# Twelve later row tiles normalised in the first part instead of six, leaf buffers fifteen instead of twelve, the second part's written order replaced

## The chip, the cores and the metric

The kernel runs on one core of one Trainium2 chip. Its engines work side by side, each through its own list of instructions in order: PE multiplies matrices (PEld, its weight load, runs beside it), ACT applies functions with a scale and an offset, DVE and POOL do elementwise arithmetic, and SP issues the transfers between DRAM and on-chip memory (DMA). Engines wait for one another through semaphores. PE writes its products into eight banks; ACT and DVE read them out, and a bank can be written again only then.

The metric is the time of one execution on the device, in microseconds (us): the median of several runs.

## The reference, cut to what matters

```python
# q, k, v: (8, 8, 576, 64); omega: (128, 64)
def phi(x):                       # x scaled by 64 ** -0.25
    h = einsum('bhsd,md->bhsm', x, omega) - sum(x * x, -1) / 2
    return exp(h - max(h, -1)) / sqrt(128)
q_p, k_p = phi(q_s), phi(k_s)
kv = einsum('bhsm,bhsd->bhmd', k_p, v); z = sum(k_p, 2)
attn = einsum('bhsm,bhmd->bhsd', q_p, kv) / (einsum('bhsm,bhm->bhs', q_p, z) + 1e-6)
x = attn with its heads side by side         # (8, 576, 512)
u = x + real(fft(fft(x, axis=1), axis=2))
un = (u - mean(u)) / sqrt(var(u) + 1e-6)     # along a row of 512
out = u + relu(un @ w_ch1) @ w_ch2           # 512 -> 2048 -> 512
```

All of it is float32. Batch and sequence together are 4608 rows of `u`.

## The kernel before

**Two parts.** The first part computes the attention, the Fourier mix (which stores `u` to the DRAM array `us`), the whole multilayer perceptron for the first 512 rows in four plain blocks of 128 rows (first layer L1235, second layer L1258), and conversions of the weights. The second part takes the other 4096 rows in eight blocks j = 0 to 7 of 512 rows with a two-level Strassen-Winograd scheme: each layer is 7 x 7 = 49 products ("leaves"). A leaf of a first layer is L1710, of a second layer L2153. Blocks 0 and 1 are worked alone, then 2 and 3, 4 and 5, 6 and 7 in pairs ("wide"), which share their weights. Every leaf of a second layer has a tile of weights `wl` of 256 KB, loaded from the array `w2l` (L2049) into one of 12 buffers (`NWL`). The sums of operand blocks that the scheme needs are additions at L1666, the ones that finish rows at L2202; each may be placed on DVE or on POOL. L2129 and its neighbours put leaf products together on DVE.

**Normalised, turned rows.** Blocks 1 to 7 need their rows normalised and transposed. A tile of 128 rows is loaded from `us`, ACT forms its mean and square sum in two passes, POOL makes the factor out of them in three tiny instructions, ACT scales, DVE transposes, and SP stores the result to an array `turned`, from which a block's fetch later reads its operand (L1091 for block 1, L1086 for wide blocks). There are two forms of this chain:

- *in the second part*: `normed` (L1096) lays out a block's tiles, `norm_of` (L1128) and `by_blocks` (L1058) make the instructions: load L1135 into one of two buffers `u`, ACT L1144 and L1149, POOL L1153 to L1155, ACT L1157, DVE L1068 into the buffer `turn`, store L1074. Blocks 1 to 7 have four tiles each.
- *in the first part*: the generator `ahead` (L1572) does the same for the tiles of the list `EARLY`: all four of block 1 and the first two of block 2. Its lines are load L1578, ACT L1582 and L1583, POOL L1585 to L1587, ACT L1589, DVE L1592, store L1594. A tile lies in one of the two buffers `kq` that hold keys and queries earlier on.

**The order.** The kernel's instructions are put into the queues by `Listing.run`. Each part is a set of streams (generators of steps). A step names its engine or engines, what it takes (buffers, banks) and what it waits for. Which stream is served next, and on which of its engines, is written out as text: `PICKS` and `BANKS` for the first part, `PICKS2` and `BANKS2` (three characters a step, one digit for each choice of bank) for the second. The generators of `ahead` are not in these lists. They are advanced by `BETWEEN`: groups of five digits, a count of placed steps and the number of a tile.

```python
            placed += 1
            while between and between[0][0] == placed:
                next(between.pop(0)[1], None)
```

At such a count the tile's next stage is put in the queues at that point: its load, its two ACT passes, its POOL triple, its scaling, its transpose, its store. An instruction that waits then holds up all that stands behind it on its engine. SP's queue is in order too.

**Work of the first part that the steps touch** (all near 350 to 420 us): attention forms `e` = exp on ACT (L650, eight instructions of 128x128), which PE transposes (L596). The Fourier mix has `y` on ACT (L906), read by PE at L933, and `bmp` (L977), which ACT copies out of a bank. The plain blocks write banks at L1235 and L1258, and ACT or DVE apply the relu (`ht`, L1221 and L1219). `u` rows are loaded at L1032.

## Time and profile before

| what | us |
| --- | --- |
| runs | 1128.26, 1128.29, 1128.4; median 1128.29 |
| the profiled execution | 1128.43 |
| its span, first to last instruction | 1126.6 |
| PE busy | 1108.2 (98%) |
| PEld busy | 1000.7 (89%) |
| DVE busy | 888.1 (79%) |
| ACT busy | 541.8 (48%) |
| POOL busy | 357.4 (32%) |
| moved by DMA | 236.11 MB, 210 GB/s over the span |

The profile is that of one execution; 1.8 us of its time lie outside the span. Busy shares are averages over parts with different limits, so the table says only that PE is nearly always at work: 18.4 us of the span are left in which it is not. The page's slices show where; its first and last lie at the start and the end of the program:

```
PE   8999999999999999999999999999999999999998
DMA  8956757565675549799899668757778756556553
```

Each digit is a fortieth of the span, 28 us, in tenths; 9 stands for 90% or more. Finer windows and the timeline of one engine follow in the prediction.

### The profile page before, as it was taken

The page shows a single profiled execution, that of the slowest core. Times are in us where ns is not written, and L with a number is a line of the kernel's source. Part 1 is how long each engine was busy: PE and PEld are TensorE (multiplying, and loading weights), DVE is VectorE, ACT ScalarE, POOL GpSimd, SP SyncE. Part 2 cuts the span into 40 slices and gives each one's busy share as a digit, 9 for nine tenths or more (in the row PEclk, how much of TensorE's full clock was granted, in tenths as well). Part 3 has the DMA queues.
Part 4 walks back from the last instruction along what each step waited for, and adds up shares of the span by engine and source line. Part 5 has one row for each costly group of instructions (what it writes and reads, how often), then busy time and mean ns, then how long its engine had stood idle before and what let it go on. Part 6 is the DMA issues. An engine that isn't in the chain of part 4 may idle for free.

```text
span 1126.6 us, 31534 instructions
## 1 busy us (share of the span) xinstructions
PE 1108.2 (98%) x12467; PEld 1000.7 (89%) x12467; DVE 888.1 (79%) x1705; ACT 541.8 (48%) x1644; POOL 357.4 (32%) x381
## 2 busy tenths in 40 slices
PE   8999999999999999999999999999999999999998
PEld 7878888879869779999999889999889999889998
DVE  6999998987577766497788777888667898668895
ACT  7998898856536335534313553223563222341221
POOL 2443443644473335434300454000365000142000
PEclk9999999999999999999999999999999999999999
DMA  8956757565675549799899668757778756556553
GB/s 236 234 178 180 238 174 211 165 206 165 219 234 183 156 137 350 209 292 293 225 317 323 188 204 267 205 151 226 214 208 258 216 152 219 167 156 215 150 157 106
DMA packets 194867, 236.11 MB, mean 210 GB/s; under 512 B 52128, under 2 KB 118944, under 8 KB 194720
## 3 DMA queue, kind: packets, MB, share of 16 engines
q1 hardware_dynamic: 194224, 233.83, 68.3%
q8 instruction: 99, 1.62, 0.6%
q14 instruction: 48, 0.39, 0.1%
q10 hardware_dynamic: 496, 0.26, 0.1%
HBM read 182.13 MB, written 56.10 MB: 211 GB/s over the span
## 4 chain that ended last, share of the span: by engine, by line
PE 90%; DMA 3%; DVE 3%; ACT 2%; SPq 1%; issue 0%; DVEq 0%; ACTq 0%
PE banks L2153 30%; PE banks L1710 27%; PE banks L690 5%; PE banks L1235 5%; PE banks L596 5%; PE banks L1258 5%; PE banks L1861 4%; PE banks L724 3%; PE banks L771 2%; PE banks L933 2%; PE banks L883 1%; DMA wl<-w2l 1%; DMA kq<-in_q_dram 1%; PE banks L893 1%; ACT e L650 1%; PE banks L944 1%
## 5 line engine op out<-in xcount | busy, mean ns | idle before, releaser
L2153 PE MATMUL banks<-wl,sums 128*128 128x128 f32 x1792 | 219.8, 275 | 0.0
L2153 PEld LDWEIGHTS banks<-wl,sums 128*128 128x128 f32 x1792 | 210.9, 192 | 0.9 <-issue 0.2
L650 ACT ACTIVATE e<-banks,nmx 128x128 f32<-128x128 f32 x576 | 165.3, 432 | 22.6 <-DVE nmx L633 22.0
L633 DVE TENSOR_REDUCE nmx<-banks 128x8 f32<-128x1024 f32 (+1 forms) x96 | 89.4, 952 | 19.1 <-PE banks L690 14.9
L2153 PE MATMUL banks<-wl,hid 128*128 128x128 f32 x768 | 99.2, 276 | 3.1 <-DMA wl<-w2l 1.8
L2153 PEld LDWEIGHTS banks<-wl,hid 128*128 128x128 f32 x768 | 92.6, 192 | 4.5 <-DVE part L2129 1.8
L2124 ACT ACTIVATE s<-banks 128x128 f32<-128x128 f32 x112 | 31.0, 277 | 121.1 <-PE banks L2153 111.5
L1710 PE MATMUL banks<-unw,wxw 128*128 128x256 f32 x352 | 85.5, 379 | 0.0
L690 PE MATMUL banks<-om,kqT 64*64 64x128 f32 (+1 forms) x2088 | 79.2, 275 | 1.5 <-ACT kv L740 0.8
L690 PEld LDWEIGHTS banks<-om,kqT 64*64 64x64 f32 (+1 forms) x2088 | 64.5, 138 | 12.7 <-issue 3.4
L2153 PE MATMUL banks<-wl,hx 128*128 128x128 f32 x576 | 74.2, 275 | 0.4 <-DVE part L2129 0.4
L1710 PEld LDWEIGHTS banks<-unw,wxw 128*128 128x128 f32 x352 | 66.6, 190 | 8.9
L1710 PE MATMUL banks<-rx,wxw 128*128 128x256 f32 x288 | 71.2, 379 | 0.0
L1710 PE MATMUL banks<-ttw,wxw 128*128 128x256 f32 x288 | 70.0, 379 | 0.0
L2153 PEld LDWEIGHTS banks<-wl,hx 128*128 128x128 f32 x576 | 69.4, 192 | 0.7 <-DVE part L2129 0.6
L1735 ACT ACTIVATE s<-banks 128x512 f32<-128x512 f32 x65 | 38.6, 595 | 60.0 <-PE banks L1710 54.8
L1235 PE MATMUL banks<-unT,w 128*128 128x128 f32 x512 | 65.4, 279 | 1.7 <-DVE qeT L610 1.7
L1235 PEld LDWEIGHTS banks<-unT,w 128*128 128x128 f32 x512 | 60.2, 192 | 4.5 <-issue 2.3
L539 POOL TENSOR_TENSOR w<-w,raw 128x512 f32<-128x512 f32 x28 | 37.4, 1343 | 76.6 <-DVE raw L533 76.6
L1710 PEld LDWEIGHTS banks<-rx,wxw 128*128 128x128 f32 x288 | 54.5, 190 | 7.3
L1710 PEld LDWEIGHTS banks<-ttw,wxw 128*128 128x128 f32 x288 | 54.5, 190 | 7.3
L1258 PE MATMUL banks<-w,ht 128*128 128x512 f32 x128 | 58.8, 598 | 0.0
(268 smaller groups left out, 2353.3 us busy)
## 6 DMA issues: line engine op xcount, KB each, us to landing
wl<-w2l SPq DMA_DIRECT2D x245, 256.0 KB
wxw<-w1x SPq DMA_DIRECT2D x120, 256.0 KB
raw<-in_moe_w_ch_dram SPq DMA_DIRECT2D x32, 512.0 KB
kq<-in_k_dram SPq DMA_DIRECT2D x32, 288.0 KB
kq<-in_q_dram SPq DMA_DIRECT2D x32, 288.0 KB
vd<-in_v_dram SPq DMA_DIRECT2D x32, 288.0 KB
u<-us SPq DMA_DIRECT2D x30, 256.0 KB
ur<-us SPq DMA_DIRECT2D x30, 256.0 KB
```

Of the source, the lines that this page charges most:

```text
L539: eng.tensor_tensor(out=dst, in0=dst, in1=lof, op=ALU.add)
L596: nc.tensor.transpose(ps[:, (j - j0) * 128 : (j - j0 + 1) * 128], src(j), ident[:])
L633: nc.vector.tensor_reduce(nmx[:, :, 0:num], pps[:, :, 0 : MF * num].rearrange("p b (c m) -> p b c m", m=MF), axis=AX.X, op=ALU.max, negate ...
L650: nc.scalar.activation(out=e[:, c + (i if num == 1 else 0), :], in_=pps[:, i, MF * c : MF * c + MF], func=AF.Exp, bias=nmx[:, i, c : c + 1],)
L690: nc.tensor.matmul(pps[cols, c, MF * m : MF * m + MF], lhsT=kqT[rows, j, cols], rhs=om2[rows, :],)
L724: nc.tensor.matmul(kvp[cols, i, 0 : D + 1], lhsT=feature(r)[rows, cols], rhs=vds[n % NV][rows, r, :], start=(r == 0), stop=(r == R - 1),)
L1235: nc.tensor.matmul(hp[:, 0:TP], lhsT=w1[:, dc, 128 * fc : 128 * fc + 128], rhs=unTs[key][:, dc, :], start=(dc == 0), stop=(dc == NDC - 1),)
L1258: nc.tensor.matmul(yp[:, 0:DM], lhsT=hs[fc][:, 128 * i : 128 * i + 128], rhs=w2[:, fc, :], start=(fc == 0), stop=(fc == NFC - 1),)
L1710: nc.tensor.matmul(ps[:, span * f : span * f + span].rearrange("f (b q) -> f b q", q=Q), lhsT=left[:, P * f : P * f + P], rhs=right, start ...
L1735: nc.scalar.activation(out=s[:], in_=ps, func=AF.Copy)
L1861: nc.tensor.matmul(cell.rearrange("f t (b q) -> f t b q", q=Q), lhsT=w[:, d, col : col + 128], rhs=right[:, :, d].rearrange("f (t b) q -> ...
L2153: nc.tensor.matmul(ps[:, 0:128], lhsT=left[:, f], rhs=wls[head(j), i, n][:, f], start=start and f == 0, stop=(f == 3), skip_group_check=True,)
```

## The change

Twelve tiles are in `EARLY`: all of blocks 1, 2 and 3. The list `PLACES` gives each of them a buffer: tiles 0, 1, 5, 6, 10 and 11 in the two `kq` buffers (`k`), tiles 2, 3, 4, 7, 8 and 9 in the three buffers of the tag `turned`, which hold turned keys in the attention (`t`). `BETWEEN` has groups for twelve tiles, the number being a hexadecimal digit, and places most stages of tiles 0 to 5 elsewhere than before. `normed` serves blocks 4 to 7 only, and its branches for blocks 1 to 3 are gone. Of the leaves of blocks 0 and 1 in the second layer, every fifth takes the place of a `u` buffer or of the `turn` buffer (`tag_of`), so that there are 12 + 2 + 1 buffers; wide blocks keep 12. The second part's order `PICKS2` and `BANKS2` is replaced whole. The first part's `PICKS` and `BANKS` stay.

In numbers of instructions: PE, ACT and SP have as many as before (of SP's, six loads and six stores come from L1578 and L1594 instead of L1135 and L1074); 21 additions of L1666 and L2202 go from DVE to POOL. PE's order is the same in the first part and in the last 1552 matmuls.

```diff
+PLACES = "kktttkktttkk"
 BETWEEN = (
-    "1662016621167001690116910169101693016991169911699117300173011750217502175031766317692176921769317773"
-    "17792177921790317903180341804518204182041820418205182051820518384183851846418465")
+    "1662016620166211670116910169101691116911169301693117300173011730217302174321743217503175031750417504"
+    "1750517506175821763217637176651766617693176931769417694176951769617713177131771817765177761777717794"
+    "17794177991785517855179061790617928179991803a1804b18057180571806818069181371813718168182091820a1820a"
+    "1820a1820b1820b1820b1824818248183491838a1838b184291846a1846b")
 PICKS2 = (
...
 BANKS2 = (
...
         def paced(i):
             h, k = divmod(i, HT // 128)
-            before, then = ((("first", j - 1, n[i], 0), "y") for n in ((1, 1, 5, 2), (6, 2, 7, 3)))
-            if wide(j):
-
-                n, was = i + TB // 128 * (j - head(j)), head(head(j) - 1)
-                order_ = [((("first",) + p), "y") for p in heads(was)]
-                at = [m * (len(order_) - 2) // 7 for m in range(8)]
-                if j <= WIDE + 1:
-                    order_ = [(("first", 0, 7, 0), "y"), *((("second", 0, k), "p1") for k in (4, 6))]
-                    order_ += [(("first", 1, ORDER1[k], 0), "y") for k in (0, 2, 4, 6)]
-                    at = range(-2, 6)
-                before, then = order_[at[n]], order_[at[n] + 1]
+
+            n, was = i + TB // 128 * (j - head(j)), head(head(j) - 1)
+            order_ = [((("first",) + p), "y") for p in heads(was)]
+            at = [m * (len(order_) - 2) // 7 for m in range(8)]
+            before, then = order_[at[n]], order_[at[n] + 1]
             yield Step(NONE, after=events_of(range(t0, t0 + TB // 128)) + (before,))
             yield from norm_of(j, t0 + 2 * h, i, pool, None, (h, k), (then,))
         for i in range(TB // 128):
-            if (j, i) in EARLY:
-                continue
-            if wide(j):
-                n = i + TB // 128 * (j - head(j))
-                was = head(head(j) - 1)
-                at = 98 * was + 49 * len(unit(was)) * n // 8 - 8
-                if j <= WIDE + 1:
-                    at = (0, 0, 28, 52, 73, 98, 112, 126)[n]
-                yield Fork(paced(i), LEAF * at)
-                continue
-            yield Fork(paced(i), LEAF * (98 * j - 60 + 8 * i))
+            n, was = i + TB // 128 * (j - head(j)), head(head(j) - 1)
+            yield Fork(paced(i), LEAF * (98 * was + 49 * len(unit(was)) * n // 8 - 8))
     def norm_of(j, t, i, pool, dst, block=None, after=()):
...
         h, k = divmod(i, HT // 128)
         t = (NPLAIN * TP + TB * j) // 128 + 2 * h
-        place = ld.tile([P, 2 * R, D], F32, name="kq", tag="kq")[:].rearrange("p c d -> p (c d)")
+        if PLACES[EARLY.index((j, i))] == "k":
+            place = ld.tile([P, 2 * R, D], F32, name="kq", tag="kq")
+        else:
+            place = att.tile([128, R, 128], F32, name="kqT", tag="turned")
+        place = place[:].rearrange("p c d -> p (c d)")
         u, w = place[:, 0:DM], place[:, DM : 2 * DM]
         nc.sync.dma_start(u, us[P * t : P * (t + 2), :].rearrange("(b k q) d -> k b q d", k=2, q=Q)[k])
         yield
...
         nc.sync.dma_start(turned_of(j, h)[:, :, k], turn.rearrange("p g d q -> p g (d q)"))
         listing.made["turned", j, i] = 0.0
-    EARLY = [(j, i) for j in (1, 2) for i in range(TB // 128)][:6]
+    EARLY = [(j, i) for j in (1, 2, 3) for i in range(TB // 128)]
     def betweens():
         tiles = [ahead(*n) for n in EARLY]
-        return [(int(BETWEEN[n : n + 4]), tiles[int(BETWEEN[n + 4])]) for n in range(0, len(BETWEEN), 5)]
+        return [(int(BETWEEN[n : n + 4]), tiles[int(BETWEEN[n + 4], 16)]) for n in range(0, len(BETWEEN), 5)]
     every = mybir.EngineType
     ctx.enter_context(
...
         return (4, 1, 2, 6, 5, 3, 7) if head(j) != head(NTB - 1) else (4, 1, 2, 6, 7, 5, 3)
+    def tag_of(j, i, l):
+
+        n = (49 * j + 7 * order(j).index(i) + PARTS.index(l)) % 15
+        if wide(j) or n % 5 != 4:
+            return "wl", NWL
+        return ("turn", 1) if n == 14 else ("u", 2)
+
     def load_leaves():
         for j in HEADS:
             for i in ORDER1[j == WIDE :] if wide(j) else ():
...
                     wxs[j, i, n] = wx
             for i in order(j):
                 for l in PARTS:
+                    tag, n = tag_of(j, i, l)
                     yield Step(
-                        SP, 0.45, 2.6, take=("wl",), after=(("w2l", i),), kb=165, makes=("wl", j, i, l),
+                        SP, 0.45, 2.6, take=(tag,), after=(("w2l", i),), kb=165, makes=("wl", j, i, l),
                         bias=due(j, 1, i) + (LEAF * 2 * PARTS.index(l) if wide(j) else 0.0) - 14,
                     )
-                    wl = late.tile([128, 4, 128], F32, name="wl", tag="wl", bufs=NWL)
+                    wl = late.tile([128, 4, 128], F32, name="wl", tag=tag, bufs=n)
                     nc.sync.dma_start(wl[:].rearrange("p f m -> p (f m)"), w2l[i][STORED.index(l)])
                     wls[j, i, l] = wl
...
                 0.895,
                 after=(("wl", head(j), i, n),) + shared + after,
                 take=take,
-                give=(() if wide(j) and j == head(j) else ("wl",)) + give,
+                give=(() if wide(j) and j == head(j) else tag_of(j, i, n)[:1]) + give,
                 makes=makes or (me, n), bias=pace * LEAF * PARTS.index(n),
             )
             b = None
...
             yield from block_norms(j, late)
     def late_turns():
-        for j in range(2, NTB):
+        for j in range(4, NTB):
             yield from normed(j, late)
     listing.run(
```

More of the change, by code (lines that the diff above doesn't have):

```diff
@@ L103 @@
 PICKS2 = (
-    "0260260270280000270290290290260280240261260290310251280251290450480490270451280230480420480290460440"
-    "2802602504812504802404704604504704504505105105103812605105002504102404912404804604604802304404904614"
-    "9150048048052053049052053053035044049046037052037041028046125037048044048038046037141154052043043060"
-    "0400370330330570540351230450370350360270440580570570470550261230420521230280360360480470400440470300"
-    "4603803504004202802905005605614815903905705312305906103405804905003705604905905403304903804803303905"
@@ L109 @@
-    "2058048051037033046051034039058051046059059025057046038033052035037055039060057043037047045054057045"
-    "0410440670571270670690530670440470400510470510490310600460390270390580380500611280630560590620410631"
-    "2715106104904706000005505005405405604315904004704314403205505305315405303204303805712615102603603914"
-    "2052040043038041153049064060053022049050040061039047063000050038040049052050051035129054022059137044"
-    "0500500370570320370200630560340480200440500471440590600600410580510360420490400550510520610471510590"
@@ L114 @@
-    "6203805106006205606005706015705805406115004216005203215606005915705105205405215604805405204804603815"
-    "6027022054049028148047043046051045053155147045047024053148043050153043046148021037047055056052037054"
-    "1490480520410430501470540470000551520470520490550571471531560470540440440540520490540480440450490320"
-    "5104603503914804704005105103204404604004304904405304704005104303304905013903905005104704005204604804"
-    "5051052053053053042145045046054141049046153040052040051051046047051048038053143147049053053053053045"
@@ L119 @@
-    "0410450240430430410001460420480270360481410440440380390500420400460440410450420310420480420520500440"
-    "4204503804205114903604003804703704004802103904504604701803903905403703605405405205605505503703403705"
-    "2055051051054053050053053050053055036029051050035051050044046048051051050046049053053046052044044034"
-    "0440480480450430470240320430460451540460460450500471490550410320400480450450000450460430390470470500"
-    "4504604104404002204904004702404504004811804004402104103604704503804004104204203502804804603404504704"
@@ L124 @@
-    "6048039039037044045042043044042034034040040045042040040039034000052032033044038033016032040027032037"
-    "0340430361250290380400330420320360370480390370460290420300350400500370251260490390170360370330410430"
-    "3303103203703603802304403803003604502403603504603303202504604103402304403403103003003202604113814103"
-    "3030032041032039026034030029127027131027036029027031041045041027029027034142143032020039037027036028"
-    "0270400400261340321270320260310310310370370350340300350300331310350340350390390390391360370260360300"
@@ L129 @@
-    "3012903703103103513113903403203303903403703203102903303602902313513402903313602403403203512803513403"
-    "2135032036033033133031030034032131030031032032132031034035128032028037032038035132032035032026026023"
-    "0300370161270251270270260360271321331360310250310290351300341311331340241330290350251320320290290180"
-    "2002201712503102102403102902402803203401803202803302503203112103012802102102203002802003102302702712"
-    "6020023026023023124023020023029017027122028027125024023026128030029024021029027021026023029027020125"
@@ L134 @@
-    "0230261210261301330250240240260240220320280220300300251250280220250190250300201200270000200260220220"
-    "2303303302602801902612402802702502401902912902802802102702402802002702602502302802102601702502102202"
-    "8018027026028020020127127127021018023024019000019025014017026027026018024026017014021016020017020016"
-    "022017016025024"
+    "0200220200000180190230220230200200240210200250240191251250230250230230230280440230220200170180420420"
+    "4302604004101801801801803512004103404003503412004104304204802303204603004502204403604303604501912004"
@@ new lines @@
+    "0031040119019031022036038030032032024045145045145049033122047036034039017047033042042048023046037045"
+    "0250360430270420190241411430421190450380360480320490330220250500500390360390410430480310340440430220"
+    "2804904402305403301803204003905304704802703101803903705303802805205303605004004304004805404903805305"
+    "3036047020046037048044117126039023032043042037024044026035044037043032051024025054019046046038119033"
+    "0530470520440350280440480280410490470471470190440420460441190460440460440480500400530310380250370380"
@@ new lines @@
+    "3903302505201904603804713504103502915004803413114803304404405014705302804002514214304314703004604702"
+    "1045043047029042029053045039052046045051029038038052050026037050049050046046049047051049041044151040"
+    "0400480430500490320210330451441350250381520440231510450290391510401530170350460430470360370500450521"
+    "4203615404804315004301604405204701905314604503804304905204714514904004201804804104114704714904404704"
+    "7050026146032020022045045036047017047045139021045028025033049042048042044035027047045031025031034040"
@@ new lines @@
+    "0380381360450320310370461460370400350420220420411301440390391390420400430220430451420440431390420380"
+    "3703703103704102203904304313803503303801603103403304104203203702403704103804204203504204104404403804"
+    "0139041037044139042040039039043036043038039033046046046046046046045033040039043136142042044040043039"
+    "0470360450310440470370420380410410420460460371370400410430440430400441250370340330340360430380360390"
+    "4003503404403903603905503905003705505505505005403404903504803514802704903204804904802004504105003105"
@@ new lines @@
+    "1048050048049052044046052043050041048044044031041042025042038016045046019040041042044037041044018049"
+    "0420460470420440390470370371420420350400360350380420450180430340400360360360350460340340390370370490"
+    "4205203404803604503503903704404304202905103404204102704003304705003504904504304804303104904704905003"
+    "0041043049036039047047047034043040042044029030038033035037041126020044036036033045034042043037041125"
+    "0440440390380480380410350310460250500450370380370310300260380350410340410450450450360440390360430430"
@@ new lines @@
+    "2803604103303903403703903504203003903603804203603603903203403403303903414013314202503202604103103913"
+    "7041031039042037038034042037031040035032035031031040131019034040131031034030026029038029039035038036"
+    "0330351320231370341311370341340270310280311311330380310391370340270280380290321360350330330380301300"
+    "2703512903703203203602813103102903313102703302703103703302703303213303413203402903613203503603602702"
+    "3127020131031134027019132032027025032033024028033128031029031021016032027029023029026033033132031127"
@@ new lines @@
+    "0270310290290270301251320190240221300301300240290310250280320270250240310281250280250271270300240220"
+    "2803003001702503002602402902002902603102202703002702902202502113113102802902802103202413002902903302"
+    "8024032017021016025026024000026030028033031029030017023024025025024029031031025030029021019027118022"
+    "0200310210330250240220281250270180230300300300300220310310270250200180000190180230210270250170180220"
+    "3002902402601801701502302202202301702402701801802802101901702302701602112001902102401801801502602702"
@@ L138 @@
+    "3021020030022028018020028015016015020015018033035032035018017019029014015027028015029015029000028030"
+    "030026025027026"
 )
 BANKS2 = (
-    "5670712567365475162765765076736574251742053164735260173564271706573527460152371054362071534267053152"
-    "76"
+    "5670512657367410557657657625754360671452603172465071374605263072645016472350473612540371645623701746"
+    "37125"
 )
```

## The prediction

> **What bounds the kernel now.** I read the windows first: the span cut into stretches, with each engine's busy time in each. The columns are: window, its length, then busy us (and instructions) of PE, PEld, DVE, ACT, POOL, the granted TensorE clock, the share of the DMA engines, GB/s.

> ```profile
> 350.00:375.00 25.00, 25.00 (x431) 20.37 (x432) 18.30 (x49) 14.59 (x52) 7.64 (x12) 1.00 0.50 175
> 375.00:400.00 25.00, 25.00 (x194) 19.68 (x189) 18.72 (x47) 10.41 (x35) 6.68 (x15) 1.00 0.44 125
> 400.00:425.00 25.00, 25.00 (x145) 16.73 (x144) 16.34 (x40) 9.34 (x23) 8.13 (x11) 1.00 0.55 159
> 475.00:500.00 25.00, 24.57 (x216) 24.03 (x214) 20.96 (x30) 7.87 (x29) 12.72 (x13) 1.00 1.01 284
> 500.00:525.00 25.00, 23.66 (x209) 23.47 (x210) 19.03 (x46) 9.27 (x24) 8.93 (x10) 1.00 0.93 277
> 575.00:600.00 25.00, 23.61 (x205) 23.16 (x204) 20.47 (x40) 4.91 (x19) 0.00 (x0) 1.00 0.97 327
> ```

> PE sets the time: it is busy 1108.2 us of a span of 1126.6, and its clock stands at 1.00. In 350 to 425, where the six added tiles go, PE never waits, and DMA stands at half. From 475 to 600, the second layers of blocks 0 and 1, PE loses 0.43 + 1.34 + 1.39 = 3.16 us, with DMA at 0.93 to 1.01: too many bytes. PE's timeline names the losses (start, length, engine, line, operation, in brackets the idle time before it and what ended it):

> ```profile
> 486.04 1.16 PE L2153 MATMUL banks<-wl,hid 128*128 128x128 f32 x8 [0.37 <-DMA wl<-w2l]
> ...
> 500.90 1.16 PE L2153 MATMUL banks<-wl,hid 128*128 128x128 f32 x8 [0.93 <-DVE part L2129]
> 502.50 2.05 PE L2153 MATMUL banks<-wl,hid 128*128 128x128 f32 x16 [0.44 <-DVE part L2129]
> ...
> 581.33 1.13 PE L2153 MATMUL banks<-wl,hid 128*128 128x128 f32 x8 [0.60 <-DMA wl<-w2l]
> ...
> 585.10 1.16 PE L2153 MATMUL banks<-wl,hid 128*128 128x128 f32 x8 [0.79 <-DMA wl<-w2l]
> ```

> They sum to 3.13 us. The two on DVE are DMA too: before them DVE sat on L1404's additions, 497.59 to 500.64, which had waited for block 1's transposed rows (L1091), queued on SP behind some 17 loads of leaves. Between 600 and 1100 no window shows PE idle; 1100 to 1125 loses 2.35 us in a tail whose last 325 DMAs and 1552 matmuls the change leaves in their order. So 3.13 us is all that the second part can gain.

> **The change, part by part.** The engine orders of the changed program are compared with those of before. PE's first 4059 matmuls, with their banks, are the same.

> *Second part.* Six tiles' loads (L1135, 256 KB), ACT passes (L1144, L1149, L1157), POOL triples, transposes (L1068) and stores (L1074, 256 KB) leave the stretch behind 475. All ran beside a full PE, so they are worth what they held up, the 3.13 us. Less goes ahead of the leaf loads: adding up SP's transfers, 39.5 MB instead of 42.9 are issued up to the leaf that was late at 581, and 12.75 instead of some 16.5 up to that at 486. With 15 buffers, the smallest lead of a leaf load in blocks 0 and 1 (matmul time between the freeing of its buffer and its use, counted in both orders) grows from 7.37 to 10.05 us; transfers of this kind in the chain of waits took 4.86, 4.29 and 3.73 us. L1404 now stands behind an earlier fetch. I take the whole gain, -3.13; the low bound is the two DVE terms and little else, -1.5.

> *First part, work.* Each tile adds to ACT 0.64 + 0.20 + 0.72 + 0.19 = 1.75 us by its rows, 1.53 where they overlap (362.04 to 363.57; below "a pair"), and 0.8 for the scaling L1589; to DVE 0.71 (L1592), to POOL three operations of 0.19 to 0.55, to SP a load and a store of about 0.57. Six tiles: 14 us of ACT, spread over three windows with 10 to 16 idle each, so the sum fits. What counts is which instruction they are put ahead of, for ACT runs in order:

> ```profile
> 360.03 2.17 ACT L650 ACTIVATE e<-banks,nmx 128x128 f32<-128x128 f32 x8
> 362.04 0.69 ACT L1582 ACTIVATE kq<-kq 128x512 bf16<-128x512 f32 x1
> ...
> 390.09 0.62 ACT L1582 ACTIVATE kq<-kq 128x512 bf16<-128x512 f32 x1
> ...
> 391.75 0.83 ACT L906 ACTIVATE y<-banks 128x256 f32<-128x256 f32 x3
> ...
> 395.96 0.40 ACT L977 ACTIVATE bmp<-banks 128x258 f32<-128x258 f32 x1
> ...
> 408.42 0.63 ACT L1582 ACTIVATE kq<-kq 128x512 bf16<-128x512 f32 x1 [1.49 <-DMA kq<-us]
> ```

> and on PE, what waits for them:

> ```profile
> 361.55 1.15 PE L596 MATMUL banks<-ident,e 128*128 128x128 f32 x9
> ...
> 393.02 0.61 PE L933 MATMUL banks<-sd_sb,y 128*128 128x129 f32 x4
> ...
> 397.65 2.84 PE L1235 MATMUL banks<-unT,w 128*128 128x128 f32 x24
> ...
> 407.34 3.17 PE L1258 MATMUL banks<-w,ht 128*128 128x512 f32 x7
> ```

> A. Tile 0's pair now stands ahead of the eight `e`, not behind them. PE's L596 at 361.55 needs the first four, which end at about 361.17, a slack of 0.38: 1.53 - 0.38 = 1.15 late, and 1.2 by the L1235 that needs the last four.
> B. Ahead of the second half of `y` (391.75) stand two pairs and a scaling, part of which falls in ACT's idle time; `y` ends about 1.5 later. L933 at 393.02 has 0.43 of slack: 1.05.
> C. Then two pairs and two scalings, one of each more, ahead of `bmp` (395.96 to 396.36), which ends near 399.5. PE's L1235 of 397.65, by then 398.7, writes the bank that `bmp` reads: 0.85.
> D. Tiles 7, 8 and 9 wait for the three turned buffers that tiles 2, 3 and 4 give back with their stores. On SP that is load, land, work, store, load. The store of tile 3 can go at about 398.95; issue to the next start on SP takes 2.7 (L1032's two `u` loads landed after 2.75 and 2.68), load of tile 8 at 401.6, store of tile 4 at 402.6, load of tile 9 at 405.3. It lands at 408.0, and ACT stands at its L1582 till then. A pair, a scaling and the `bmp` of 404.88 follow: to 410.65. L1258 at 407.34, by then 409.24, needs that bank: 1.4. Bounds: 0.2, if the stores go out as the data is ready; 5.4, if the load takes as long as the row of 408.42 (issued 401.68, 6.7 us).

> Behind D the first part's last stores and the loads of block 0 meet a queue that is ahead of need. Sum of A to D: 1.2 + 1.05 + 0.85 + 1.4 = 4.5. Bounds: 0, if all is absorbed as the pair at 390.09 is now (no gain: PE is full there), and 8.5, with D at 5.4.

> *Additions.* 21 of L1666 and L2202 go from DVE (0.69) to POOL (1.27). POOL has room (0 to 13 of 25 us a window), DVE gains 14 us. I take 0; the high bound is a rival.

> Sum: 1128.43 + 4.5 - 3.13 = 1129.80. The profiled execution stands 0.14 above the median of 1128.29, so by the median 1129.7. Its own range, with C and D between half and one and a half of their size and the gain between 2 and 3.13: 1127.6 to 1131.0.

> **Rivals.**

> *The stalls do not come (faster).* PE shows no wait in 350 to 425 with six tiles, and ACT is idle 58% of 375 to 400. Against: the slacks are 0.4 us and a pair is 1.5. Then 1128.29 - 3.13 = 1125.2.

> *Late load (slower).* The turn of D: one load, tile 9's, at the head of ACT's queue. For it: in 400 to 425 ACT already waited 1.49 us so, for a load that took 6.7. It decides from a load longer than about 4 us on: then D is up to 5.4, and 1129.7 + 4.0 = 1133.7. Against: DMA is at 0.55 there. [...]

> *POOL in DVE's way (slower).* L1666's rows: on DVE 0.648 to 1.751 us, median 0.686; on POOL 1.265 to 1.778, median 1.272. So one beside the other can cost DVE 1.06 more. Eight of the moved additions lie near 546 to 571, where DVE is busy 22 of 25 us: up to 8 x 1.06 = 8.5 us of DVE time, against 3 us of room in 550 to 575 and 14 us taken off DVE elsewhere. About 2.5 us could reach PE's second layer of block 1: 1132.2. Against: most L1666 rows are at the median. [...]

> *The change does not do what it says* (DMA near 575 still full, leaves still late): the stalls come without the gain: 1132.8; little speaks for it, since the bytes do move.

> **How the numbers follow.** Less than 0.2% (2.3 us) is no change that a measurement of this kernel can tell. Forecast 0.46, of which 0.43 within 0.2% and 0.03 above it; no stalls 0.21 (faster); late load 0.13, POOL 0.12 and the change without its gain 0.08, all slower. So faster 0.21, same 0.43, slower 0.36. The range leaves out the ends of both sides: 1125.1 to 1133.2.

> **What would show it.** In the changed profile: PE waits on ACT's `e` near 361, `y` near 394, `bmp` near 399 and 409, the last with ACT idle on the DMA of tile 9's rows; windows 350 to 425 short by 4.5 us in all. From 475 to 600 no wait of L2153 on `wl` or on L2129, and DMA below 0.93. Wrong: PE still full from 350 to 425 (then it is faster), a wait over 3 us near 409, or waits on DVE behind POOL's L1666 from 546 on.

## The result, and the profile after

| | before | after |
| --- | --- | --- |
| median of 5 runs, us | 1128.29 (1127.54 to 1128.59) | 1146.39 (1145.81 to 1148.8) |
| ratio, 95% interval | | 1.0163 (1.0149 to 1.0178) |
| span of the profiled execution | 1126.6 | 1144.0 |
| PE busy | 1108.2 | 1115.0 |

The kernel is slower by 18 us. Since PE runs the same matmuls of the first part in the same order, one can subtract the start of a given matmul in one trace from its start in the other. The difference stands at 0.6 us at 357, at 21.1 at 434 (times of the kernel before) and at 17.4 from 619 to the end. So the first part lost 20.5 us, all within 80 us, and the second part gained 3.7.

The 25-us windows of the changed kernel, in the columns of the prediction:

```profile
350.00:375.00 25.00, 23.97 (x371) 19.08 (x371) 17.30 (x42) 14.38 (x49) 5.87 (x9) 1.00 0.45 157
375.00:400.00 25.00, 19.23 (x185) 14.03 (x180) 16.14 (x43) 9.79 (x33) 6.37 (x11) 0.91 0.48 152
400.00:425.00 25.00, 20.07 (x151) 18.79 (x149) 8.26 (x25) 12.66 (x34) 9.45 (x23) 0.81 0.40 116
425.00:450.00 25.00, 23.33 (x95) 14.42 (x96) 16.71 (x38) 12.50 (x26) 9.08 (x13) 0.93 0.72 212
...
500.00:525.00 25.00, 25.00 (x226) 25.00 (x225) 20.55 (x35) 5.21 (x22) 8.19 (x6) 1.00 0.98 306
575.00:600.00 25.00, 24.70 (x221) 24.52 (x221) 21.42 (x34) 3.30 (x15) 9.27 (x7) 1.00 1.02 296
```

From 500 to 600 PE is all but full, and behind 465 it waits 0.8 us in all (0.5 and 0.3), where the kernel before waited 3.1: the gain came. DMA, at 0.98 and 1.02, did not fall below 0.93 as the prediction expected. From 350 to 450 PE idles 13.4 us, no engine is near its limit, and the granted clock drops. PE's timeline has four waits there (lines have moved: L601 was L596, L1161 was L1171, L1225 was L1235, L1248 was L1258, L1572 was L1578):

```profile
363.32 1.20 PE L601 MATMUL banks<-ident,e 128*128 128x128 f32 x9 [1.03 <-ACT e L655]
399.39 1.09 PE L1161 MATMUL banks<-ident,u 128*128 128x128 f32 x4 [5.77 <-DVE u L1157]
411.67 1.16 PE L1225 MATMUL banks<-unT,w 128*128 128x128 f32 x8 [2.86 <-DVE ht L1209]
426.67 15.55 PE L1248 MATMUL banks<-w,ht 128*128 128x512 f32 x32 [3.75 <-ACT bmp L982]
```

The chain of waits says what DVE and ACT were late for (start, us, what):

```profile
383.62 12.43 DMA u<-us
...
400.10 3.20 DMA turned<-kqT
...
403.35 5.81 DMA kqT<-us
...
410.42 5.86 DMA kqT<-us
...
417.65 6.18 DMA kqT<-us
```

A plain load of rows, 2.7 us in other places, took 12.43. The three loads into refilled buffers took about 6 us each, and each stood on SP until the store that frees its buffer had landed: from the store's issue to the start of the load took 3.25 us (400.10 to 403.35), 4.91 (405.51 to 410.42) and 6.11 (411.54 to 417.65). The plain load behind the first of them (issued at 403.97) reached DVE at 409.72, and the `ht` that PE's wait of 2.86 was for stands behind it on DVE. Two finer windows show why, and what followed:

```profile
384.00:386.00 2.00, 2.00 (x11) 1.28 (x10) 2.00 (x4) 1.15 (x3) 1.17 (x2) 1.00 0.26 99
...
396.00:402.00 6.00, 2.60 (x13) 2.63 (x14) 4.29 (x11) 1.45 (x4) 3.18 (x8) 0.50 0.36 125
```

While the loads of tiles 2 to 6 are under way, DMA stands at 0.26 and 99 GB/s: the time of about four of sixteen engines. A load of L1572 is 128 packets of 2 KB, 87 ns each in this trace; over four engines that is 2.8 us. The load's source is written as four groups of 32 rows. Five such loads, with one plain load among them, are 14 us at that rate, an estimate (5 x 2.8); in the trace DMA does not fall below the time of four engines from 381 to 395.5. The plain load behind them, issued at 383.62, landed in sixteen parts: twelve by 388.29, the last four from 395.02 to 396.05, just after the four last ones of the load issued at 380.94 (394.43 to 395.41). So its last quarter came behind these loads. Whether the four groups of rows are why they ran so is tested by e1.

The second window shows the clock at 0.50. It is at half from 395.7 to 402.5, from 412.8 to 419.6 and from 426.4 to 429.8. The matmuls of L1225 start 213 ns apart there (412.9 to 419.5), where they start 112 ns apart at 1.00 (403 to 408). PE works in 3.1 + 6.8 + 3.1 us of that and so loses half, 6.5 us. The account: waits 1.03 + 5.77 + 2.86 + 3.75 = 13.4, clock 6.5, together 19.9 of the 20.5.

### The profile page after: what moved, and what is told of

It reads as the page before. It is cut to its first block, busy times and chain, and to the rows that moved or that the text cites. A ratio compares the mean times of both kernels' runs of the same rounds, so it can differ in the third digit from the quotient of the medians.

```text
span 1144.0 us, 31517 instructions
## 1 busy us (share of the span) xinstructions
PE 1115.0 (97%) x12467; PEld 1006.3 (88%) x12467; DVE 891.3 (78%) x1684; ACT 539.8 (47%) x1644; POOL 387.7 (34%) x402
## 4 chain that ended last, share of the span: by engine, by line
PE 86%; DMA 6%; DVE 4%; ACT 2%; issue 1%; SPq 0%; ACTq 0%; DVEq 0%
PE banks L2155 30%; PE banks L1704 26%; PE banks L601 5%; PE banks L695 5%; PE banks L1248 4%; PE banks L1855 4%; PE banks L1225 3%; PE banks L729 3%; PE banks L776 2%; DMA kqT<-us 2%; PE banks L938 1%; PE banks L888 1%; ACT e L655 1%; DMA u<-us 1%; DVE nmx L638 1%
## 5 line engine op out<-in xcount | busy, mean ns | idle before, releaser
L2155 PE MATMUL banks<-wl,sums 128*128 128x128 f32 x1792 | 219.8, 275 | 0.5 <-issue 0.5
L2155 PEld LDWEIGHTS banks<-wl,sums 128*128 128x128 f32 x1792 | 210.7, 192 | 1.5 <-issue 0.9
L2155 PE MATMUL banks<-wl,hid 128*128 128x128 f32 x768 | 99.1, 275 | 0.3 <-DVE part L2131 0.3
L2155 PEld LDWEIGHTS banks<-wl,hid 128*128 128x128 f32 x768 | 92.9, 192 | 0.9 <-DVE part L2131 0.5
L2155 PE MATMUL banks<-wl,hx 128*128 128x128 f32 x576 | 74.2, 275 | 0.4 <-DVE part L2131 0.4
L1225 PE MATMUL banks<-unT,w 128*128 128x128 f32 x512 | 68.4, 286 | 4.6 <-DVE ht L1209 2.9
L2155 PEld LDWEIGHTS banks<-wl,hx 128*128 128x128 f32 x576 | 69.5, 192 | 0.8 <-DVE part L2131 0.6
L1225 PEld LDWEIGHTS banks<-unT,w 128*128 128x128 f32 x512 | 62.8, 198 | 7.6 <-DVE ht L1209 3.0
L1248 PE MATMUL banks<-w,ht 128*128 128x512 f32 x128 | 60.4, 612 | 3.7 <-ACT bmp L982 3.7
L2204 POOL TENSOR_TENSOR more<-more,part 128x512 f32<-128x512 f32 x2 | 2.6, 1314 | 175.6 <-ACT part L2197 175.6
```

The source lines that it names most:

```text
L1225: nc.tensor.matmul(hp[:, 0:TP], lhsT=w1[:, dc, 128 * fc : 128 * fc + 128], rhs=unTs[key][:, dc, :], start=(dc == 0), stop=(dc == NDC - 1),)
L1248: nc.tensor.matmul(yp[:, 0:DM], lhsT=hs[fc][:, 128 * i : 128 * i + 128], rhs=w2[:, fc, :], start=(fc == 0), stop=(fc == NFC - 1),)
L2155: nc.tensor.matmul(ps[:, 0:128], lhsT=left[:, f], rhs=wls[head(j), i, n][:, f], start=start and f == 0, stop=(f == 3), skip_group_check=True,)
```

## The experiments

Theory F: the form of the loads (four engines) and SP's order made the losses. Rival O: the order on ACT did, as steps B and C had it. T: the store-to-load turns of step D. The kernel before ran beside each set, with medians of 1129.1 (e1 to e4), 1130.3 (e5 to e8) and 1130.4 (e9 to e11); its runs spread wider there (1125.5 to 1134.8), so what is read in the traces is the loss of the first part, between the same two matmuls as above (356 and 434), and the gain of the second (434 to 619).

**e1.** All orders stay; the load of `ahead` is split:

```diff
-        nc.sync.dma_start(u, us[...].rearrange("(b k q) d -> k b q d", k=2, q=Q)[k])
+        rows = us[...].rearrange("(b k q) d -> k b q d", k=2, q=Q)[k]
+        for b in range(4):
+            nc.sync.dma_start(u[Q * b : Q * b + Q], rows[b])
```

> The changed kernel, but each of the twelve loads of L1572 is issued as four transfers of 32 rows; all orders stay. Theory F (few engines): in the changed kernel's trace these loads run at about 96 to 100 GB/s with a DMA share of 0.26, that is on four of sixteen engines, some 2.8 us each (128 packets of 87 ns over four); the five of tiles 2 to 6 keep the plain u load of 383.62 from landing until 396.07. Spread, that load lands before 390: the wait of L1161 on DVE falls from 5.77 us to below 1.0; from load to ACT's pair takes 3.5 to 4.5 us instead of 5.9 to 6.3, so the waits of L1225 (2.86) and L1248 (3.75) fall by 1.5 to 2.5 each and most of the half-clock stretches go: 1129 to 1135. Theory O (order on ACT, steps B and C of the prediction): the pairs ahead of y set the stall, the wait near 394 to 399 stays above 4 us, and the time stays at 1143 to 1147.

Measured: 1135.14 us, ratio 1.0044 (1.0024 to 1.0064). First part -9.7 us instead of -20.5, second part +3.4. PE's timeline of e1:

```profile
393.62 0.63 PE L1161 MATMUL banks<-ident,u 128*128 128x128 f32 x4 [0.68 <-ACT kqT L1578]
400.51 2.05 PE L1225 MATMUL banks<-unT,w 128*128 128x128 f32 x16 [0.52 <-ACT bmp L982]
403.86 1.16 PE L1225 MATMUL banks<-unT,w 128*128 128x128 f32 x8 [1.30 <-DVE ht L1209]
...
414.30 14.00 PE L1248 MATMUL banks<-w,ht 128*128 128x512 f32 x32 [1.41 <-ACT bmp L982]
```

5.77 became 0.68, and the clock is 1.00 from 375 to 475. From 382 to 387.6, while SP issues split loads, DMA moves some 149 GB/s, not 99: the form of the load set its rate. F holds, though 1135.14 is just outside what it expected: SP took 1.7 to 1.8 us, once 3.5, to issue four transfers. Small waits are left. The profile puts the 0.68 down to ACT, but the operand `u` of that matmul was finished on DVE (L1157) at 393.47, late because its load was issued only at 387.56 and reached DVE at 390.29: this is the price of issuing. The 0.52 on `bmp` is step C's. Ahead of the 1.30 stands a plain load behind a refill (issued at 399.06), ahead of the 1.41 ACT's wait of 2.49 us for a refill: both belong to the turns of step D. O explains the 0.52, not the large waits.

**e2.** `BETWEEN`: the loads of tiles 5 and 6 move from step 1750 to 1754.

> The changed kernel, but on SP the loads of tiles 5 and 6 stand behind the second plain u load and the ur load, not ahead of them; nothing else moves on any engine. Theory F: the u load has two of these loads less ahead of it, 2 x 2.8 = 5.6 us, and lands near 390.5: the wait of L1161 falls from 5.77 to 1.0 or less, its half clock (about 1.6) goes too: 1138 to 1141. Theory O: nothing changes, 1145 to 1148.

Measured: 1141.05 us (1140.13 and 1141.97), ratio 1.0100 (1.0063 to 1.0138), at the upper end of what F expected. Two transfers moved in one queue took the large wait away, with the wait on `bmp` from 3.75 to 2.67, while that of L1225 grew from 2.86 to 4.38. O, for which nothing changed here, falls as the cause of the large wait. PE in e2:

```profile
391.73 0.63 PE L1161 MATMUL banks<-ident,u 128*128 128x128 f32 x4 [0.67 <-ACT kqT L1576]
...
405.07 2.08 PE L1225 MATMUL banks<-unT,w 128*128 128x128 f32 x8 [4.38 <-DVE ht L1209]
```

**e3.** `BETWEEN`: loads of tiles 7 and 8 to step 1778, of 9 to 1790; their ACT passes, POOL triples and scalings to 1820, transposes and stores after.

> The changed kernel, but the loads of tiles 7 and 8 stand on SP behind the last plain u load, that of tile 9 behind the store of tile 6, and the passes of tiles 7 to 9 on ACT, POOL and DVE behind the last relu of the plain part. Theory T (turns, step D): the waits of L1225 (2.86) and L1248 (3.75) go, with about 5 us of half clock behind them, and the 5.77 of L1161 stays: 1133 to 1137. If SP's store-to-load turns were not what holds the u loads up, both waits stay: 1144 to 1147. A third way: the five tiles now in a row on ACT delay the second part's first leaves; then PE waits for ACT after 425, 2 to 6 us.

Measured: 1142.62 us (1141.25 and 1144.0), ratio 1.0114 (1.0075 to 1.0153). The large wait stayed at 5.52, both turn waits went, and new ones came where the second part starts:

```profile
400.36 1.09 PE L1161 MATMUL banks<-ident,u 128*128 128x128 f32 x4 [5.52 <-DVE u L1157]
436.11 1.16 PE L1704 MATMUL banks<-tt,w1s 128*128 128x128 f32 x8 [0.57 <-DVE tt L1347]
438.66 1.16 PE L1704 MATMUL banks<-unT,w 128*128 128x128 f32 x8 [1.17 <-ACT banks L1736]
442.36 1.16 PE L1704 MATMUL banks<-unT,w1s 128*128 128x128 f32 x8 [1.65 <-ACT s L1729]
```

The time is well above what T alone expected. T and the third way are both true: the turns made the waits of 2.86 and 3.75, and five tiles in a row at the end of the first part cost 6.2 us at the second part's start.

**e4.** The order stays, the leaf tiles are allotted from one tag of 12 buffers (`tag="wl", bufs=NWL`).

> The changed kernel in its own order, but the leaf tiles of blocks 0 and 1 go round 12 buffers, not 15. If the second part gained by the bytes that left it, its gain stays: from the last matmul of the first part to the end as in the changed kernel within 0.3 us. If it gained by the buffers, each load can start three leaves (about 6.7 us) later, leads fall to 3 to 8 us, and L2155 waits on wl again: 2 to 8 us slower than the changed kernel.

Measured: 1148.16 us (1147.47 and 1148.85). The first part lost 20.4 as the changed kernel, the second gained 1.5 instead of 3.7. So 2.2 us of the gain come from the three buffers. The other 1.5 come from the bytes and the new order of the second part together, which no run takes apart. The waits of e4 behind 470 (waiting instruction, releaser: us in total, times, longest):

```profile
PE banks L2155 <- DVE sums L1660: 1.2, 1, 1.2
PE banks L2155 <- DMA wl<-w2l: 1.1, 1, 1.1
```

**e5 and e6.** The kernel before, with three loads added on SP behind the load of tile 3, into idle buffers; e5 in one transfer each, e6 in four.

```diff
+    def more(n):
+        place = att.tile([128, R, 128], F32, name="kqT", tag="turned")[:].rearrange("p c d -> p (c d)")
...
+        nc.sync.dma_start(place[:, 0:DM], rows)
```

> The kernel before with one addition: on SP, behind the load of tile 3 and ahead of the second plain u load, three more loads of the form of L1578 into the buffers turned; nothing reads them and no other engine has a new instruction. Theory F: they take three times 2.8 us on the same four engines, the u load lands 8.4 us later than its 386.9, near 395.3, and PE, whose L1171 stood at 391.64 with 1 to 2 us of slack behind that load, waits 3 to 5 us there, with 1.6 to 5 us of half clock behind it: 1132 to 1138. Theory O: no pair was moved, so nothing changes: 1127.5 to 1129.5.

> As the run with three loads added to the kernel before, but each of the three issued as four transfers of 32 rows: the same bytes, nine more transfers on SP (some 4 us of issuing). Theory F: spread over all engines they hold the u load up by the issuing and some 3 us of transfer, not 8.4: the wait at L1171 is 0 to 2 us, 1128 to 1131. If it were the bytes or the count of transfers ahead of the u load, it is as slow as the other, or slower.

Measured: e5 1140.41 us, ratio 1.0087 (1.0064 to 1.0111); e6 1136.52, 1.0054 (1.0036 to 1.0072). SP, DVE and PE of e5, then of e6:

```profile
383.64 2.44 SPq L1032 DMA_DIRECT2D u<-us  x1
397.49 0.69 DVE L1161 BATCH_NORM_STATS2 st<-u 128x6 f32<-128x512 f32 x1 [9.20 <-DMA u<-us]
400.82 1.09 PE L1171 MATMUL banks<-ident,u 128*128 128x128 f32 x4 [7.22 <-DVE u L1167]
```

```profile
378.41 10.57 SPq L1603 DMA_DIRECT2D kqT<-us  x12
389.08 0.36 SPq L1032 DMA_DIRECT2D u<-us  x1
391.81 0.69 DVE L1161 BATCH_NORM_STATS2 st<-u 128x6 f32<-128x512 f32 x1 [6.53 <-DMA u<-us]
395.13 1.09 PE L1171 MATMUL banks<-ident,u 128*128 128x128 f32 x4 [4.55 <-DVE u L1167]
```

In e5, with no instruction added outside SP, the `u` load took some 11 us from the end of its issue at 386.1 to 397.5, and PE waited 7.22 us at L1171. Wait and time are more than expected. That shows the mechanism by itself. In e6 the same load, behind the same bytes, took 2.7 us, as expected, but was issued at 389.08: the twelve transfers kept SP for 10.57 us where e5's three took 2.01, 8.6 us more and not 4, and PE waited 4.55. So e6 missed its 1128 to 1131. In the profiled executions its first part lost 8.7 us (10.2 us of half clock included; at 1139.25 this execution is slower than the median), hardly less than the 9.0 of e5. The transfer itself tells the two forms apart, 2.7 us against 11, and the time hardly does. Splitting the transfers was not free here; the price, 8.6 us for three of them, was paid in the queue.

**e7 and e8.** The changed kernel's second part, with every stage of the twelve tiles put where the trace of the kernel before shows its engine idle: loads of 2 to 4 at step 1730, their pairs at 1733, of 5 and 6 at 1762, pairs at 1766 and 1777, refilled buffers' loads behind the plain ones, tiles 8 to 11 at 1820. e7 with split loads, e8 with the old ones.

> The changed kernel's second part, twelve tiles in its buffers, loads of four transfers, and every stage of the twelve tiles put into a stretch in which the trace of the kernel before shows its engine idle: the pairs of tiles 2, 3, 4 in ACT's idle time from 382.3 to 388.1, tile 5's at 393, 6's at 397, 7's at 401, those of 8 to 11 behind the last relu; tiles 0 and 1 as in the kernel before; the refilled buffers' loads behind the plain u loads. If order and loads are all that the first part lost by, it loses 0 to 2 us there and keeps the second part's 3.4 to 3.7: 1124.5 to 1127, faster than both kernels. If twelve tiles are too much for the first part wherever they stand, PE waits for ACT or POOL at the start of the second part, 3 to 6 us, as in the run without turns: 1128 to 1132.

> As the run with the stages respaced, but each load one transfer, as in the changed kernel. Theory F: three loads stand ahead of one plain u load and two more behind it, so tiles 3 and 4 land 5 to 8 us later than when spread, past their stretch on ACT, and y behind their pairs is late: a wait of 2 to 5 us near 393, with half clock; 1129 to 1136. If the form of the load matters only where five stand in a row, it is within 1 us of the run with spread loads.

Measured: e7 1129.95 us, ratio 1.0001 (0.9987 to 1.0015); e8 1135.74, 1.0050 (1.0033 to 1.0067). Spacing with split loads took the first part's loss to 4.5 us, where 0 to 2 were expected, with the old loads to 11.4. The loss of e8 is not where it was expected: the refilled last tile held ACT for 6.61 us, and PE's largest wait, 4.14, is at the second part's start. The other reading, that the form matters only where five such loads stand in a row, falls. ACT and PE of e8:

```profile
423.63 0.63 ACT L1576 ACTIVATE kq<-kq 128x512 bf16<-128x512 f32 x1 [6.61 <-DMA kq<-us]
428.55 1.97 PE L1704 MATMUL banks<-unT,w 128*128 128x128 f32 x8 [4.14 <-ACT banks L1736]
```

In e7 PE and ACT show the two faults left:

```profile
406.48 0.66 PE L1161 MATMUL banks<-ident,u 128*128 128x128 f32 x4 [1.30 <-ACT bmp L982]
```

```profile
426.95 0.60 ACT L1731 ACTIVATE s<-banks 128x512 f32<-128x512 f32 x1 [2.35 <-DMA out_dram<-ur]
```

A pair and a scaling were put behind a relu instead of ahead of it, and ACT, like DVE, waited for the store of the last plain rows, which stood on SP behind the stores of tiles 7 to 11.

**e9.** As e7, with tiles 7 to 9 in buffers that `e` leaves free, so that no load waits for a store, and with the two faults mended.

```diff
-PLACES = "kktttkktttkk"
+PLACES = "kktttkkeeett"
...
+        if at == "e":
+            u, w = (att.tile([P, 4, MF], F32, name="e", tag="e", bufs=NE)[:] ... for _ in range(2))
```

> As the respaced run, but tiles 7, 8 and 9 lie in buffers that the attention's e has left, so that no load waits for a store on its way; the loads of 7 and 8 stand ahead of the third plain u load, the pairs of 7 and 8 in ACT's idle time from 400.6 to 403.8, and the scaling of 6 alone ahead of the last bmp. The respaced run lost 1.3 us at L1161 to a pair and a scaling put after a relu, and 3 us from 427 on, where ACT and DVE waited for the store of the last plain rows, which stood on SP behind the stores of tiles 7 to 11. If these two are all, the first part loses 0 to 1 and the second part's gain of 3.4 stays: 1125 to 1127 against the kernel before on the same chip at 1128 to 1130, 2.5 to 3.5 us faster. If the second part's new order itself starts slower, the waits of L1857 near 432 and 436 (0.6 and 0.8) stay and the gain is 1 to 2 us.

Measured: 1124.83 us (10 runs), ratio 0.9954 (0.9937 to 0.9971): 5.6 us under the kernel before beside it, where 2.5 to 3.5 were expected. The windows of e9:

```profile
350.00:375.00 25.00, 25.00 (x445) 20.20 (x444) 18.68 (x51) 14.87 (x54) 8.87 (x14) 1.00 0.49 171
375.00:400.00 25.00, 25.00 (x172) 19.83 (x170) 18.61 (x46) 15.96 (x46) 8.91 (x22) 1.00 0.73 206
400.00:425.00 25.00, 25.00 (x144) 16.65 (x143) 19.20 (x45) 15.96 (x36) 11.49 (x20) 1.00 0.75 205
425.00:450.00 25.00, 25.00 (x127) 22.24 (x126) 17.81 (x17) 13.11 (x23) 23.55 (x16) 1.00 1.00 357
```

With all twelve tiles in it, the first part has no wait: 0.1 us lost, ACT at 16 of 25. The waits of L1857 at the second part's start are gone too. So the changed kernel's idea is worth its gain, and all of the loss lay in where the stages stand, in which buffers, and how the loads are written. The traces account for 2.9 of the 5.6 us, the second part's gain up to 619. The rest is not shown; the kernel before may lose more in some executions than in its profiled one, for e5, e6 and e11 have its second part and lost another 0.4, 2.9 and 4.5 us there.

**e10.** e9 with the leaves in 12 buffers, as in e4.

> The run without refills, but the leaves go round 12 buffers in the same order. The buffers were worth 2.2 us in the changed kernel; if that holds where PE is on time, this is 1.5 to 3 us slower than the run without refills, with waits of L2157 for wl or for sums between 475 and 520; if buffers mattered only because the first part was late, it is within 0.5 us.

Measured: 1128.71 us, ratio 0.9989 (0.9972 to 1.0005). The second part gains 1.4 instead of 2.9 up to 619; it waits 1.46 us for `wl` and 0.96 for sums:

```profile
483.30 1.16 PE L2162 MATMUL banks<-wl,sums 128*128 128x128 f32 x8 [0.96 <-DVE sums L1667]
496.74 2.02 PE L2162 MATMUL banks<-wl,sums 128*128 128x128 f32 x16 [1.46 <-DMA wl<-w2l]
```

So by the traces the three buffers are worth 1.5 us here. By the medians of the two, run in one set, it is 3.9; what makes up the difference is not shown.

**e11.** The kernel before with four more ACT passes ahead of tile 2's pair.

```diff
+        for _ in range(4 if (j, i) == EARLY[2] else 0):
+            nc.scalar.activation(out=junk, in_=u, func=AF.Identity, scale=-1.0 / DM)
```

> The kernel before with four more passes of L1582's kind, without a sum, on ACT ahead of tile 2's pair, and so ahead of the second half of y: 4 x 0.62 = 2.5 us, less the 0.43 us of slack of L933 makes a wait of 2.1 us on ACT's y at 393.0, step B's rule. If the clock is granted by how long PE idles, and some 2.7 us are needed for half speed (waits of 1.4 kept the clock, 2.67 and 2.86 lost it), the clock stays at 1.00 and the time is 2 us more than before: about 1130.3 where before is 1128.3. If shorter idling is enough, half clock follows for 3.4 us or a multiple, and 1.7 to 5 us more.

Measured: 1133.44 us, ratio 1.0025 (1.0007 to 1.0042). PE and the windows of e11:

```profile
392.84 0.71 PE L933 MATMUL banks<-sd_sb,y 128*128 128x129 f32 x4 [1.87 <-ACT y L906]
```

```profile
393.50:400.30 6.80, 6.80 (x38) 6.55 (x37) 1.21 (x4) 3.49 (x10) 1.43 (x4) 0.50 0.00 0
400.50:405.00 4.50, 4.50 (x46) 4.35 (x45) 3.61 (x13) 0.94 (x3) 2.94 (x5) 1.00 0.65 188
```

Step B's rule gave 2.1 and 1.87 came. But half clock followed for 6.8 us: in this execution a wait of 1.9 us cost 5.3. It is the slowest of the ten, at 1136.53; the median lies 3.0 us above that of the kernel before.

## Why the prediction was wrong

It forecast +1.4 us, within 0.2%; +18 came. The first part was to lose 4.5 us by steps A to D and lost 20.5. Two steps failed: the price of a turn in D, and the reading of the DMA share as room, which put the added loads at nothing but their issue. The clock came on top of both.

- *Second part.* Forecast -3.13, measured -3.7; the waits of 486, 501 to 502, 581 and 585 are gone. Right, with the buffers as a cause by themselves (e4, e10); bytes and order are not taken apart. "All that the second part can gain" was too little, since waits cost PE more than their brackets here: in the kernel before, counted from start to start less the bracket, the matmul ahead of the wait of 500.90 takes 275 ns and the one behind it 213, where most take 112. That is some 0.26 us more.
- *A.* Forecast 1.2, measured 1.03. Right.
- *B and C.* In the changed kernel they are hidden behind the larger wait. With the loads spread (e1) C's L1225 waits 0.52 where 0.85 was forecast. B's matmul, now L938, shows no wait there: held up by the 0.68 of L1161, it starts at 395.10, as `y` ends (395.05). e11 shows B's rule by itself. Right in kind; C was somewhat too large, B's size in the changed kernel is not shown.
- *D.* The mechanism was right, the size was not. The step that failed is "issue to the next start on SP takes 2.7 (L1032's two `u` loads landed after 2.75 and 2.68)": the turn was priced with a load of another form. The row of the load's own form, 6.7 us, stood in the same paragraph as a bound. Measured are 5.81, 5.86 and 6.18 for the loads and 3.25, 4.91 and 6.11 from a store's issue to the next load's start, and waits of 2.86 and 3.75 in place of 1.4. The rival of the late load, with a chance of 0.13, is the one that came true, in three loads where it had priced one.
- *The wait of 5.77 was not forecast at all.* The step behind it is the first reading, "DMA stands at half" in 350 to 425, together with the cost of an added load as 0.57 us on SP. A mean over sixteen engines does not tell whether four of them are full. The trace of before showed it: DMA at 0.23 to 0.26 from 378 to 382, with two `kq` loads under way, and the plain `u` load behind them, issued at 381.70, reaching DVE after 5.2 us (386.93), not 2.7. e1, e2 and e5 show that this is the cause.
- *The clock.* The prediction's sum has no term for it. At 0.50 for 6.8, 6.8 and 3.4 us, it cost 6.5 us.
- *POOL in DVE's way* did not happen: behind 470 PE waits 0.8 us in all, none of it for POOL. In e1, e3, e7 and e8 PE does wait 0.8 us for an addition on POOL (`so`), once, between 436 and 451. *The stalls do not come* fell, though e9 shows that it can be had.
- *The inner range* does not follow from its terms: half to one and a half of C and D, with a gain of 2 to 3.13, give 1128.6 to 1132.0, not 1127.6 to 1131.0. Neither holds 1146.4.

## What to carry to other kernels

Price a transfer by the row of its own form and by the engines that it uses, not by its bytes against a mean: loads written as four groups of rows ran at 0.26 of sixteen engines here, and the plain load behind them in the queue landed after 12.43 us instead of 2.7. An instruction put into a full schedule is priced by the slack of what stands behind it on its engine, and a PE wait by more than its length, since after some waits here the clock stood at 0.50 for 3.4 to 10.2 us (next section). Where a stretch has idle time on every engine and PE still waits, move the stages and not the work.

## What the runs showed of the hardware

Half clock came after short waits and lasted one, two or three times some 3.4 us. After 1.87 us (e11) it was at half for 6.8 us, after 2.67 and 4.38 (e2) for 3.4 and 10.2, after 2.86, 3.75 and 5.77 (the changed kernel) for 6.8, 3.4 and 6.8, after 5.52 (e3) for 10.2. After 1.30 and 1.41 (e1) it stayed at 1.00, but near 504 in e11 waits of 1.19 and 0.44 brought 3.4 us of it (506.2 to 509.6), and at the start of the kernel before a wait of 2.79 us for a `kq` load (7.13 to 9.92) brought none. So the length of a wait did not decide in these runs.
